# Weight sums spread over the second chunk, high parts moved to ScalarE, and PSUM banks exchanged in a two-mixer kernel

## The chip, the cores and the metric

The kernel runs on one core of a Trainium2 chip. The metric is the device time of one execution in microseconds; of several executions the median is given. The engines are named TensorE (PE in the profile, its weight loads PEld), VectorE (DVE), ScalarE (ACT), GpSimd (POOL) and SyncE (SP, whose queue issues the DMAs).

## What is computed

A linear attention, then two mixers, on a batch of 4 with 576 tokens of 512 channels. Inputs q, k, v are float32; most of the weights arrive as 64-bit floats.

```python
# attention: phi(x) = concat(exp(x@w_phi - m), exp(-(x@w_phi - m))), m = max|x@w_phi|
x  = num / den                                   # 4 x 576 x 512
# first mixer
u  = x + (x^T @ U @ V)^T                         # rank 32 over tokens
x  = u + max(u @ w_ch1, 0) @ w_ch2               # 512 -> 2048 -> 512
# second mixer
u  = x + (max(x^T @ w_tok1, 0) @ w_tok2)^T       # 576 -> 256 -> 576 over tokens
x  = u + max(u @ w_ch1', 0) @ w_ch2'             # 512 -> 1536 -> 512
```

## The kernel before

Every product is made of three matmuls. Each float32 operand is split (`split`, L94 to L98 with `cp` and `sub`) into a high part, a cast to fp32r (CAST, L96 on ScalarE or L98 on VectorE), and a low part, the subtraction of the cast from the operand (L101, on VectorE or POOL); a product is high x high, high x low and low x high, added up in a PSUM bank. The letters "a", "v", "p" in the calls of `split` choose ScalarE, VectorE or POOL.

The 64-bit weights are decoded on the chip by `load64`: a DMA brings a raw tile, ScalarE converts its two halves (L144 and L145), VectorE puts exponent, mantissa and sign together (L147, L150); the result, a tile w, is then split and its staging buffers become free.

The kernel has three phases.
- The attention with the token mix of the first mixer and 5 of the 16 slices of its channel part (to about 422 us). Its last results leave PSUM by `xT<-yp` (L498).
- The other 11 slices for eight half batches, `channel` (about 422 to 770 us): per slice a first product hp_b (12 matmuls of 288 columns), `relu_split` (L185 on ScalarE writes hhb, the high part; L186 on VectorE writes hlb, the low part) and the second product yb (12 matmuls into four banks). After each batch `tokmix2` does the token part of the second mixer (gp, gh, m2p).
- The channel part of the second mixer, `channelC`, called for five chunks of 256, 512, 512, 512 and 512 columns, named c0 to c4. The 12 slices of 128 hidden channels are taken in six pairs. The first chunk is plain: `one(p)` makes two first products hpc per pair, two relus, and `second(p)` multiplies them into the banks of yc. The other chunks go by `seven(p)`: the four products of a 2 x 2 block scheme are replaced by seven products of half the size (into banks named xc, yc, zc, vc), whose operands are parts of the activations (t0c to t6c, made by `token_mats` from uc) and weights or sums of weights. hbc, hac and u2c (L815 to L824) add the seven results together before the relus.

The weights of the pairs are loaded by `pair_weights`, while the second phase ends and chunk c0 runs: sh and sl hold seven high and low parts for a pair, vh and vl those of the second product. Entries 3 to 6 hold sums of weights: for the first two pairs (EARLY = 2) most are made in `pair_weights` (s, L672), for the others in `sums(p)` (s, L703, with casts on ScalarE and subtractions on VectorE), which before is called in chunk c0 after each pair. Its results are first read in chunk c1.

The order of instructions on each engine is set by the framework's scheduler, which lays them out ahead of time by its own estimates; `tc.issue_after(x)` keeps what is inside from standing ahead of x in that order. `gates` holds the two relu instructions behind which `token_mats` of a later chunk is laid. PSUM has eight banks; a pool that is opened first gets the lower ones, so the order of the pools psy (yc, yb, m2p: four banks), psh (hp_b, hpc, xc, yc's seven-product Y: two banks) and psg (two banks) decides which banks of the attention phase (psk bank 0, psx banks 1 to 5, psm 6 and 7) each gets.

Of the kernel before, what the change touches and what calls it, by code (L numbers as in the profile page):

```python
# [16 lines left out]
PSUM = bass.MemoryType.PSUM  # L17
# [14 lines left out]
NF2 = 12  # L32
# [5 lines left out]
EARLY = 2  # L38
# [51 lines left out]
def body(ctx, tc, kq, vd, w_phi, U, V, wm1, wt1, wt2, wm2, out):  # L90
# [12 lines left out]
    def split(src, hi, lo, eh, el):  # L103
        cp(eh, hi, src)
        sub(el, lo, src, f32(hi))
# [396 lines left out]
    for g in range(B * NPAIR):  # L502
        r = 5 * g
# [22 lines left out]
    for b in range(B):  # L526
        r = span * b + 5 * (NPAIR - 1) + O_TM
# [17 lines left out]
    with tc.using_default_side("right"):  # L545
# [1 line left out]
        extra.append(BX.enter_context(tc.tile_pool(name="rawx", bufs=RAWX, reuse_waits="tile")))  # L547
        bc = BX.enter_context(tc.tile_pool(name="bc", bufs=1, reuse_waits="tile"))
        b2 = BX.enter_context(tc.tile_pool(name="b2", bufs=2, reuse_waits="tile"))
    psy = ctx.enter_context(tc.tile_pool(name="psy", bufs=1, space=PSUM, reuse_waits="tile"))  # L550
    PB = ExitStack()
    psh = ctx.enter_context(tc.tile_pool(name="psh", bufs=2, space=PSUM, reuse_waits="tile"))
    psg = PB.enter_context(tc.tile_pool(name="psg", bufs=1, space=PSUM, reuse_waits="tile"))

    nB = NF1 - NA
# [69 lines left out]
    for t in range(NT):  # L625
        w = load64(wt1[:, t], P, 256, f"t1_{t}")
# [3 lines left out]
    for j in range(2):  # L630
        for k in range(2):
            sl = slice(k * N, (k + 1) * N)
# [46 lines left out]
    def pair_weights(p):  # L679
        sh, sl = [wc[p].tile([P, 7, 256], F32R, name=f"{t}{p}") for t in ("sh", "sl")]  # L680
        vh, vl = [wc[p].tile([P, 2, C], F32R, name=f"{t}{p}") for t in ("vh", "vl")]
        wa = loadc(2 * p, 0, p).rearrange("p (a k) -> p a k", a=2)
        split(wa, sh[:, 0:2], sl[:, 0:2], "a", "p")
        wb = loadc(2 * p + 1, 0, p)
        for k, i in enumerate((6, 2)):
            split(wb[:, k * 256 : (k + 1) * 256], sh[:, i], sl[:, i], "v", "p")
        if p < EARLY:
            sums3(p, wa, wb, sh, sl)
        for i in range(2):
            w = loadc(2 * p + i, 1, p)  # L690
            split(w, vh[:, i], vl[:, i], "av"[i], "pv"[i])
        return sh, sl, vh, vl

    wC = [pair_weights(p) for p in range(NF2 // 2)]
# [57 lines left out]
    gates = []  # L752
# [5 lines left out]
    def channelC(sl_, nm, plain):  # L758
# [4 lines left out]
        if plain:  # L763
            uh, ul = [pt.tile([P, NC, HM], F32R, tag=f"t{5 + i}", name=f"u{i}{nm}")[:, :, :n] for i in range(2)]
            split(u, uh, ul, "a", "v")
        else:
            with tc.issue_after(gates[0]), tc.issue_after(gates[1]):
                m = token_mats(u, h, nm)
        res = []
        for i in range(2):  # L770
            r = stc.tile([P, 2, 2 * HM], F32, tag="raw", name=f"res{nm}_{i}")[:, :, :n]
# [4 lines left out]
        def one(p):  # L776
            sh, sl = wC[p][:2]
            hs = []
            for i in range(2):
                hp = psh.tile([P, 512], F32, tag="m", name=f"hp{nm}_{p}_{i}")[:, :n]  # L780
                g = []
                for c in range(NC):
                    k = ((0, 1), (6, 2))[i][c // 2]
                    cs = slice((c % 2) * P, (c % 2 + 1) * P)
                    g += [(sh[:, k, cs], uh[:, c]), (sh[:, k, cs], ul[:, c]), (sl[:, k, cs], uh[:, c])]
                group(hp, g)
                hh, hl = hidden(2 * p + i, n, f"{nm}_{p}_{i}")
                r = relu_split(hp, hh, hl)
                if p == 3:
                    gates[:] = r  # L790
                hs.append((hh, hl))
            return hs

        def product(o, w, wi, ti, start):
# [8 lines left out]
        def seven(p):  # L803
            w = wC[p]
            pm = f"{nm}_{p}"
            X, Y = [psh.tile([P, 512], F32, tag="m", name=f"{t}{pm}")[:, :h] for t in ("x", "y")]
            Z, V = [psc.tile([P, 512], F32, tag=t, name=f"{t}{pm}")[:, :h] for t in ("z", "v")]
            product(X, w, 0, 0, True)
            e = pc.tile([P, HM], F32, tag="e", name=f"e{pm}")[:, :h]
            cp("a", e, X)  # L810
            product(Y, w, 4, 4, True)
            product(Z, w, 3, 3, True)
            product(V, w, 5, 5, True)
            u2 = pc.tile([P, HM], F32, tag="u2", name=f"u2{pm}")[:, :h]
            nc.vector.tensor_add(u2, Y, e)  # L815
            hb = pc.tile([P, 2 * HM], F32, tag="hb", name=f"hb{pm}")[:, :n]
            nc.vector.tensor_add(hb[:, h:], V, u2)
            nc.vector.tensor_add(hb[:, h:], Z, hb[:, h:])
            product(X, w, 1, 1, False)
            product(V, w, 2, 6, False)  # L820
            product(Z, w, 6, 2, False)
            nc.vector.tensor_add(hb[:, :h], V, u2)
            ha = pc.tile([P, HM], F32, tag="ha", name=f"ha{pm}")[:, :h]
            nc.vector.tensor_add(ha, Z, u2)  # L824
            (ah, al), (bh, bl) = hs = [hidden(2 * p + i, n, f"{pm}_{i}") for i in range(2)]
            relu_split(X, ah[:, :h], al[:, :h])
            relu_split(ha, ah[:, h:], al[:, h:])
            relu_split(hb, bh, bl)
            return hs

        def second(p, hs):
# [8 lines left out]
        prev = None  # L840
        for p in range(NF2 // 2):
            hs = one(p) if plain else seven(p)
            if plain:
                sums(p)
            if prev is not None:
                second(*prev)
            prev = (p, hs)
# [70 lines left out]
```

## Time and profile before

| what | value |
|---|---|
| median of 3 runs | 1084.78 us (1083.85 to 1087.3) |
| profiled execution | 1084.62 us |
| its span on the core | 1082.6 us |
| mean granted TensorE clock | 0.985 |
| TensorE busy | 1028.5 us, 95% of the span |
| VectorE busy | 673.5 us, 62% |
| ScalarE busy | 448.8 us, 41% |
| POOL busy | 238.7 us, 22% |

The profile records one execution. A time line gives for each group of like instructions the start, the busy time, engine, source line, operation, output and inputs and, in brackets, how long the engine was idle just before and whose end released it. The granted clock is a share of TensorE's full 2.4 GHz; half of it is the lower level of 1.2 GHz. Span and run differ by 2.0 us, which lie outside what the engines record.

### The profile page before, as it was taken

The page shows a single profiled execution, that of the slowest core. Times are in us where ns is not written, and L with a number is a line of the kernel's source. Part 1 is how long each engine was busy: PE and PEld are TensorE (multiplying, and loading weights), DVE is VectorE, ACT ScalarE, POOL GpSimd, SP SyncE. Part 2 cuts the span into 40 slices and gives each one's busy share as a digit, 9 for nine tenths or more (in the row PEclk, how much of TensorE's full clock was granted, in tenths as well). Part 3 has the DMA queues.
Part 4 walks back from the last instruction along what each step waited for, and adds up shares of the span by engine and source line. Part 5 has one row for each costly group of instructions (what it writes and reads, how often), then busy time and mean ns, then how long its engine had stood idle before and what let it go on. Part 6 is the DMA issues. An engine that isn't in the chain of part 4 may idle for free.

```text
span 1082.6 us, 17812 instructions
## 1 busy us (share of the span) xinstructions
PE 1028.5 (95%) x6960; PEld 952.2 (88%) x6960; DVE 673.5 (62%) x1221; ACT 448.8 (41%) x1049; POOL 238.7 (22%) x186
## 2 busy tenths in 40 slices
PE   8988999999989898999999999999988999999998
PEld 6767899899879787999999999998887889889887
DVE  7788987998898598743223223328899663543633
ACT  6676666756565566532112112114663221312211
POOL 3216565545545234100000000003240000000000
PEclk9998999999999999999999999999999999999999
DMA  7452323232221487410200200202753011030201
GB/s 213 151 157 58 102 56 92 71 98 71 75 78 24 128 283 230 153 60 22 89 23 22 88 22 2 88 1 80 245 157 108 1 64 55 1 117 1 78 2 39
DMA packets 62340, 92.16 MB, mean 85 GB/s; under 512 B 14512, under 2 KB 42928, under 8 KB 62256
## 3 DMA queue, kind: packets, MB, share of 16 engines
q1 hardware_dynamic: 62256, 91.03, 26.9%
q8 instruction: 54, 0.88, 0.3%
q14 instruction: 30, 0.25, 0.1%
HBM read 71.99 MB, written 18.95 MB: 84 GB/s over the span
## 4 chain that ended last, share of the span: by engine, by line
PE 69%; DVE 14%; ACT 6%; DMA 6%; issue 3%; POOL 2%; SPq 0%; DVEq 0%; ACTq 0%; POOLq 0%
PE yc L108 13%; PE yb L108 11%; PE hp_b L108 11%; PE hp_a L108 4%; PE yp L108 3%; PE pp L108 3%; PE zc L108 3%; PE vc L108 3%; PE kvp L108 3%; PE xc L108 3%; PE gp L108 2%; PE nm L108 2%; PE m2p L108 2%; PE dT L361 2%; DVE w_b L147 1%
## 5 line engine op out<-in xcount | busy, mean ns | idle before, releaser
L186 DVE SCALAR_TENSOR_TENSOR hlb<-hp_b,hhb 128x288 fp32r<-128x288 f32 x88 | 40.0, 456 | 158.5 <-ACT hhb L185 158.5
L185 ACT ACTIVATE hhb<-hp_b 128x288 fp32r<-128x288 f32 x88 | 36.1, 410 | 204.3 <-PE hp_b L108 201.6
L108 PE MATMUL hp_b<-uhb,wh_b 128*128 128x288 f32 x352 | 104.6, 299 | 3.4 <-DVE xT L498 3.4
L108 PE MATMUL hp_b<-ulb,wh_b 128*128 128x288 f32 x352 | 104.6, 297 | 0.0
L108 PE MATMUL hp_b<-uhb,wl_b 128*128 128x288 f32 x352 | 104.6, 297 | 0.0
L108 PE MATMUL yb<-hlb,wh_b 128*128 128x288 f32 x352 | 97.6, 297 | 2.1 <-DVE hlb L186 2.0
L108 PE MATMUL yb<-hhb,wl_b 128*128 128x288 f32 x352 | 97.1, 295 | 0.0
L101 POOL TENSOR_TENSOR sl<-w_c,sh 128x256 fp32r<-128x256 f32 (+1 forms) x18 | 23.8, 1340 | 332.2 <-DVE sh L98 292.1
L108 PE MATMUL yc<-hlc,vh 128*128 128x512 f32 (+1 forms) x240 | 88.3, 373 | 0.0
L108 PE MATMUL yc<-hhc,vl 128*128 128x512 f32 (+1 forms) x240 | 88.2, 372 | 0.0
L108 PE MATMUL yc<-hhc,vh 128*128 128x512 f32 (+1 forms) x240 | 81.9, 377 | 0.1
L101 POOL TENSOR_TENSOR qel<-qe,qeh 128x640 fp32r<-128x640 f32 (+1 forms) x48 | 71.3, 1496 | 25.9 <-ACT qeh L96 10.8
L108 PEld LDWEIGHTS hp_b<-uhb,wh_b 128*128 128x128 f32 x352 | 66.7, 190 | 4.8 <-DVE xT L498 3.6
L108 PEld LDWEIGHTS yb<-hlb,wh_b 128*128 128x128 f32 x352 | 66.1, 188 | 3.1 <-DVE hlb L186 3.0
L108 PE MATMUL yb<-hhb,wh_b 128*128 128x288 f32 x352 | 68.1, 296 | 0.6 <-ACT hhb L185 0.5
L108 PEld LDWEIGHTS hp_b<-ulb,wh_b 128*128 128x128 f32 x352 | 66.9, 190 | 0.1
L108 PEld LDWEIGHTS hp_b<-uhb,wl_b 128*128 128x128 f32 x352 | 66.7, 190 | 0.0
L108 PEld LDWEIGHTS yb<-hhb,wl_b 128*128 128x128 f32 x352 | 66.3, 188 | 0.0
L293 DVE TENSOR_REDUCE km<-pp 128x4 f32<-128x512 f32 x80 | 54.6, 683 | 13.4 <-PE pp L108 13.1
L101 POOL TENSOR_TENSOR kel<-ke,keh 128x512 fp32r<-128x512 f32 x36 | 48.6, 1361 | 64.2 <-ACT keh L96 62.7
L101 DVE TENSOR_TENSOR kd<-pp,km 128x512 f32<-128x512 f32 x80 | 54.4, 682 | 0.7
L108 PEld LDWEIGHTS yb<-hhb,wh_b 128*128 128x128 f32 x352 | 53.8, 188 | 1.1 <-ACT hhb L185 1.1
(249 smaller groups left out, 3056.5 us busy)
## 6 DMA issues: line engine op xcount, KB each, us to landing
raw_c<-in_wm_dram SPq DMA_DIRECT2D x24, 512.0 KB, 4.4
raw_b<-in_wm_dram SPq DMA_DIRECT2D x22, 512.0 KB, 4.6
kq<-in_kq_dram SPq DMA_DIRECT2D x80, 128.0 KB, 2.2
raw_a<-in_wm_dram SPq DMA_DIRECT2D x10, 512.0 KB, 4.3
rec<-rD SPq DMA_DIRECT2D x32, 144.0 KB, 3.2
uD<-xT SPq DMA_DIRECT2D x8, 576.0 KB, 3.4
sD<-xT SPq DMA_DIRECT2D x8, 576.0 KB, 5.3
x<-sD SPq DMA_DIRECT2D x8, 576.0 KB, 5.1
```

The costliest lines, as they stand in the source:

```text
L101: return ENG[e].tensor_tensor(out=o, in0=a, in1=b, op=ALU.subtract)
L108: nc.tensor.matmul(o, l, r, start=start, stop=stop, skip_group_check=True)
L147: nc.vector.scalar_tensor_tensor(out=wi, in0=wi, scalar=3, in1=r, op0=ALU.logical_shift_left, op1=ALU.bitwise_or)
L185: a = nc.scalar.activation(hh, hp, AF.Relu)
L186: v = nc.vector.scalar_tensor_tensor(out=hl, in0=hp, scalar=0.0, in1=f32(hh), op0=ALU.max, op1=ALU.subtract)
L293: nc.vector.tensor_reduce(out=m, in_=pv, op=ALU.max, axis=AX.X, apply_absolute_value=True)
L361: nc.tensor.transpose(tp[:, o : o + r], ds["q", g, t][:r, j, :], ident[:r, :r])
```

## The change

Five edits:
1. The pool psh is opened ahead of psy: the first products hp_b get banks 0 and 1, yb and yc banks 2 to 5. Before it was 4 and 5, and 0 to 3.
2. In `pair_weights` the casts of the second weight tile's two halves (sh entries 6 and 2) and of the second vh tile go to ScalarE. Before they were on VectorE. The subtractions stay where they were.
3. In chunk c0 `sums(p)` is called for the first two pairs only. Those of pairs 2 to 5 are queued in chunk c1, each in `seven(p - 2)` behind the last two relus of that pair.
4. The gates are taken anew in each chunk at pair 3 and dropped after use, so that `token_mats` of a chunk stands behind pair 3 of the chunk just in front. Before, those of chunk c0 served for all chunks.
5. In `one` the gates are set after both slices of pair 3.

```diff
--- before.py
+++ after.py
@@ -547,9 +547,9 @@
         extra.append(BX.enter_context(tc.tile_pool(name="rawx", bufs=RAWX, reuse_waits="tile")))
         bc = BX.enter_context(tc.tile_pool(name="bc", bufs=1, reuse_waits="tile"))
         b2 = BX.enter_context(tc.tile_pool(name="b2", bufs=2, reuse_waits="tile"))
-    psy = ctx.enter_context(tc.tile_pool(name="psy", bufs=1, space=PSUM, reuse_waits="tile"))
     PB = ExitStack()
     psh = ctx.enter_context(tc.tile_pool(name="psh", bufs=2, space=PSUM, reuse_waits="tile"))
+    psy = ctx.enter_context(tc.tile_pool(name="psy", bufs=1, space=PSUM, reuse_waits="tile"))
     psg = PB.enter_context(tc.tile_pool(name="psg", bufs=1, space=PSUM, reuse_waits="tile"))
 
     nB = NF1 - NA
@@ -683,12 +683,12 @@
         split(wa, sh[:, 0:2], sl[:, 0:2], "a", "p")
         wb = loadc(2 * p + 1, 0, p)
         for k, i in enumerate((6, 2)):
-            split(wb[:, k * 256 : (k + 1) * 256], sh[:, i], sl[:, i], "v", "p")
+            split(wb[:, k * 256 : (k + 1) * 256], sh[:, i], sl[:, i], "a", "p")
         if p < EARLY:
             sums3(p, wa, wb, sh, sl)
         for i in range(2):
             w = loadc(2 * p + i, 1, p)
-            split(w, vh[:, i], vl[:, i], "av"[i], "pv"[i])
+            split(w, vh[:, i], vl[:, i], "a", "pv"[i])
         return sh, sl, vh, vl
 
     wC = [pair_weights(p) for p in range(NF2 // 2)]
@@ -766,6 +766,7 @@
         else:
             with tc.issue_after(gates[0]), tc.issue_after(gates[1]):
                 m = token_mats(u, h, nm)
+            gates.clear()
         res = []
         for i in range(2):
             r = stc.tile([P, 2, 2 * HM], F32, tag="raw", name=f"res{nm}_{i}")[:, :, :n]
@@ -786,9 +787,9 @@
                 group(hp, g)
                 hh, hl = hidden(2 * p + i, n, f"{nm}_{p}_{i}")
                 r = relu_split(hp, hh, hl)
-                if p == 3:
-                    gates[:] = r
                 hs.append((hh, hl))
+            if p == 3:
+                gates[:] = r
             return hs
 
         def product(o, w, wi, ti, start):
@@ -825,7 +826,12 @@
             (ah, al), (bh, bl) = hs = [hidden(2 * p + i, n, f"{pm}_{i}") for i in range(2)]
             relu_split(X, ah[:, :h], al[:, :h])
             relu_split(ha, ah[:, h:], al[:, h:])
-            relu_split(hb, bh, bl)
+            r = relu_split(hb, bh, bl)
+            if p == 3:
+                gates[:] = r
+            if nm == "c1" and p + 2 < NF2 // 2:
+                with tc.issue_after(r[0]), tc.issue_after(r[1]):
+                    sums(p + 2)
             return hs
 
         def second(p, hs):
@@ -840,7 +846,7 @@
         prev = None
         for p in range(NF2 // 2):
             hs = one(p) if plain else seven(p)
-            if plain:
+            if plain and p < EARLY:
                 sums(p)
             if prev is not None:
                 second(*prev)
```

What the scheduler makes of it is shown at three places.

VectorE in the middle of chunk c1, before. hlc1_1_1 means the low part for chunk c1, pair 1, second slice; s3 and s4 are sums of pairs 3 and 4, ttc2 and uc2 the parts of chunk c2:
```order
L736 TENSOR_TENSOR ttc2_10565<-uc2_10560 128x512
L817 TENSOR_TENSOR hbc1_1_10110<-vc1_1_10081,u2c1_1_10108 128x256
L703 TENSOR_TENSOR s3_2_9755<-s3_1_9751 128x256
L736 TENSOR_TENSOR uc2_10560<-uc2_10560 128x2x256
L818 TENSOR_TENSOR hbc1_1_10110<-zc1_1_10080,hbc1_1_10110 128x256
L703 TENSOR_TENSOR s3_2_9755<-s3_2_9755,s3_0_9750 128x256
L703 TENSOR_TENSOR s3_1_9751<-s3_0_9750,s3_1_9751 128x256
L101 TENSOR_TENSOR sl3_9383<-s3_2_9755,sh3_9382 128x256
L703 TENSOR_TENSOR s3_0_9750<-s3_0_9750,s3_2_9755 128x256
L101 TENSOR_TENSOR sl3_9383<-s3_2_9755,sh3_9382 128x256
L101 TENSOR_TENSOR sl3_9383<-s3_1_9751,sh3_9382 128x256
L703 TENSOR_TENSOR s4_0_9826<-sh4_9428,sl4_9429 128x512
```
Three more rows of sums follow, and then hlc1_2_0, which empties the bank of xc1_2.

VectorE at the same place of chunk c1, after:
```order
L186 SCALAR_TENSOR_TENSOR hlc1_1_1_10083<-hbc1_1_10056,hhc1_1_1_10082 128x512
L703 TENSOR_TENSOR s3_0_10090<-sh3_9382,sl3_9383 128x512
L703 TENSOR_TENSOR s3_1_10091<-sh3_9382,sl3_9383 128x256 x2
L816 TENSOR_TENSOR u2c1_2_10162<-yc1_2_10133,ec1_2_10142 128x256
L186 SCALAR_TENSOR_TENSOR hlc1_1_0_10081<-hac1_1_10078,hhc1_1_0_10080 128x256
L186 SCALAR_TENSOR_TENSOR hlc1_2_0_10189<-xc1_2_10132,hhc1_2_0_10188 128x256
L703 TENSOR_TENSOR s3_2_10095<-s3_1_10091 128x256
L818 TENSOR_TENSOR hbc1_2_10164<-vc1_2_10135,u2c1_2_10162 128x256
L703 TENSOR_TENSOR s3_2_10095<-s3_2_10095,s3_0_10090 128x256
L703 TENSOR_TENSOR s3_1_10091<-s3_0_10090,s3_1_10091 128x256
L819 TENSOR_TENSOR hbc1_2_10164<-zc1_2_10134,hbc1_2_10164 128x256
```
The sums of pair 3 now start behind hlc1_1_1, with hlc1_2_0 after their first rows, and ttc2 has left this place; it stands behind u2c1_4.

ScalarE and VectorE at the end of the second phase, as a difference (- before, + after). The names are without their numbers of pair: hhb_1_7 and hlb_1_7 are the relu of slice 7 in the last half batch, sh the high parts of a pair of chunk weights. First ScalarE:
```order
 L96 CAST sh_9280<-w_c_0_9286 128x512
+L185 ACTIVATE hhb_1_7_8912<-hp_b_1_7_8899 128x288
 L144 ACTIVATE w_c_1_9318<-raw_c_1_9316 128x512
-L185 ACTIVATE hhb_1_7_8912<-hp_b_1_7_8899 128x288
 L145 ACTIVATE r_c_1_9319<-raw_c_1_9316 128x512
+L96 CAST sh_9280<-w_c_0_9296 128x256 x2
 L96 CAST sh_9280<-s_9306 128x256 x2
+L185 ACTIVATE hhb_1_8_8941<-hp_b_1_8_8928 128x288
```
The casts have come in, one relu has moved ahead of a decode and the next one ahead of another.

VectorE at the same place:
```order
 L147 SCALAR_TENSOR_TENSOR w_c_0_9296<-w_c_0_9296,r_c_0_9297 128x512
 L150 SCALAR_TENSOR_TENSOR w_c_0_9296<-raw_c_0_9294,w_c_0_9296 128x512
-L98 CAST sh_9280<-w_c_0_9296 128x256 x2
+L186 SCALAR_TENSOR_TENSOR hlb_1_7_8913<-hp_b_1_7_8899,hhb_1_7_8912 128x288
 L672 TENSOR_TENSOR s_9306<-w_c_0_9296 128x256
-L186 SCALAR_TENSOR_TENSOR hlb_1_7_8913<-hp_b_1_7_8899,hhb_1_7_8912 128x288
 L672 TENSOR_TENSOR s_9306<-s_9306,w_c_0_9286 128x256
```
The two casts and a sum no longer stand between the decode and hlb.

ScalarE in the plain chunk c0, where hhc_2_1 is the relu of pair 2, second slice:
```order
-L185 ACTIVATE hhc_2_1_9670<-hpc_2_1_9657 128x256
 L96 CAST sh_9428<-w_c_0_9434 128x512
 L145 ACTIVATE r_c_1_9457<-raw_c_1_9454 128x512
+L185 ACTIVATE hhc_2_1_9670<-hpc_2_1_9657 128x256
+L96 CAST sh_9428<-w_c_0_9444 128x256 x2
 L144 ACTIVATE w_c_1_9466<-raw_c_1_9464 128x512
 L145 ACTIVATE r_c_1_9467<-raw_c_1_9464 128x512
```
The relu stands two places later, and the casts of the weights behind it.

## Rows read from the trace of the kernel before

**Rows 1.** The page's busy line: busy us (share of span) xinstructions of each engine.
```profile
PE 1028.5 (95%) x6960; PEld 952.2 (88%) x6960; DVE 673.5 (62%) x1221; ACT 448.8 (41%) x1049; POOL 238.7 (22%) x186
```
**Rows 2.** Stretches: length, busy us (xinstructions) of each engine, PEclk, DMA share, GB/s.
```profile
768.00:820.00 52.00, 47.80 (x368) 44.93 (x367) 47.92 (x84) 30.82 (x59) 23.59 (x16) 1.00 0.52 164
820.00:866.00 46.00, 41.26 (x252) 36.52 (x251) 34.12 (x91) 13.18 (x34) 0.00 (x0) 0.96 0.18 58
841.50:845.50 4.00, 4.00 (x19) 3.67 (x19) 4.00 (x11) 1.90 (x7) 0.00 (x0) 0.57 0.01 4
866.00:1083.00 217.00, 212.35 (x1309) 189.31 (x1308) 98.06 (x203) 46.28 (x99) 0.00 (x0) 0.99 0.13 44
```
**Rows 3.** Waits of PE, 735 to 866 us: total us, times, longest us.
```profile
PE xc L108 <- DVE hlc L186: 3.6, 2, 2.8
PE hpc L108 <- DVE hlc L186: 2.3, 3, 1.3
PE yb L108 <- DVE hlb L186: 1.5, 2, 1.0
PE zc L108 <- DVE t3c L101: 1.3, 1, 1.3
```
**Rows 4.** Time line of PE in chunk c1: start us, us, instruction [idle before <-releaser].
```profile
840.51 0.50 PE L108 MATMUL xc<-t0c,sh 128*128 128x256 f32 x2 [2.80 <-DVE hlc L186]
...
854.82 0.40 PE L108 MATMUL yc<-t4c,sh 128*128 128x256 f32 x2
...
855.53 1.10 PE L108 MATMUL yc<-hhc,vh 128*128 128x512 f32 x4
856.46 0.40 PE L108 MATMUL xc<-t1c,sh 128*128 128x256 f32 x2
```
**Rows 5.** Time line of DVE in chunk c1.
```profile
830.44 1.34 DVE L703 TENSOR_TENSOR s<-sh,sl 128x512 f32<-128x512 f32 x3
834.21 0.69 DVE L736 TENSOR_TENSOR ttc<-uc 128x512 f32<-128x512 f32 x1 [2.42 <-DMA uc<-u2D]
...
838.43 0.68 DVE L703 TENSOR_TENSOR s<-sh,sl 128x512 f32<-128x512 f32 x1
...
840.04 0.41 DVE L186 SCALAR_TENSOR_TENSOR hlc<-xc,hhc 128x256 fp32r<-128x256 f32 x1
```
**Rows 6.** Groups by shape, 725 to 866 us: busy us, mean ns | idle before.
```profile
L96 ACT CAST sh<-s 128x256 fp32r<-128x256 f32 x24 | 9.4, 404 | 20.1 <-DVE s L703 15.3 <-DVE s L672 4.6
L96 ACT CAST vh<-w_c 128x512 fp32r<-128x512 f32 x6 | 3.7, 618 | 2.2 <-DVE w_c L150 2.0
L98 DVE CAST sh<-w_c 128x256 fp32r<-128x256 f32 x12 | 3.4, 325 | 0.8 <-PE yb L108 0.7
L98 DVE CAST vh<-w_c 128x512 fp32r<-128x512 f32 x6 | 2.7, 451 | 0.0
```
**Rows 7.** Time line of DVE in chunk c0: casts of weight halves.
```profile
785.28 0.97 DVE L98 CAST sh<-w_c 128x256 fp32r<-128x256 f32 x2
...
796.48 0.48 DVE L98 CAST sh<-w_c 128x256 fp32r<-128x256 f32 x2
```
**Rows 8.** Time line of POOL at the same two places.
```profile
784.60 1.30 POOL L101 TENSOR_TENSOR sl<-w_c,sh 128x512 fp32r<-128x512 f32 x1 [8.49 <-ACT sh L96]
...
796.84 1.87 POOL L101 TENSOR_TENSOR sl<-w_c,sh 128x256 fp32r<-128x256 f32 x2 [0.83 <-DVE sh L98]
```
**Rows 9.** Time line of PE at the start of the second phase.
```profile
425.37 0.61 PE L108 MATMUL hp_b<-uhb,wh_b 128*128 128x288 f32 x1 [3.40 <-DVE xT L498]
...
431.28 0.40 PE L108 MATMUL yb<-hlb,wh_b 128*128 128x288 f32 x1 [0.50 <-DVE hlb L186]
```
**Rows 10.** Time line of ACT there: the first relu.
```profile
428.85 0.40 ACT L185 ACTIVATE hhb<-hp_b 128x288 fp32r<-128x288 f32 x1
```
**Rows 11.** Time line of DVE there.
```profile
429.19 1.67 DVE L150 SCALAR_TENSOR_TENSOR w_b<-raw_b,w_b 128x512 int32<-128x512 int32 x1
430.78 0.81 DVE L186 SCALAR_TENSOR_TENSOR hlb<-hp_b,hhb 128x288 fp32r<-128x288 f32 x2
```

## The prediction

> **What bounds the kernel now.** I read the page's busy line first [rows 1]: TensorE is busy 1028.5 us of a span of 1082.6 us, VectorE 673.5 and ScalarE 448.8. So the matmuls set the time, and an edit gains only what it takes out of TensorE's idle time or out of time at a reduced clock. The profiled execution took 1084.62 us, 0.16 below the median of 1084.78, so a sum made against it stands for the median too.
>
> Then I asked where the idle time lies. All that the change moves is issued after about 735 us, with one exception at the start of the second phase (below). In the table of stretches [rows 2] the last 217 us, chunks two to four of the channel mixer, have TensorE at 98% (212.35 of 217.00): nothing is to be had there, and the order there hardly changes. The plain chunk (768 to 820 us) has 47.80 of 52.00, and VectorE is busy 47.92 of the same 52.00, POOL 23.59 and ScalarE 30.82. The second chunk's first part (820 to 866) has 41.26 of 46.00. So some 9 us of idle TensorE lie in these two stretches.
>
> The waits of TensorE there [rows 3] name VectorE nearly every time: xc behind hlc (3.6 us in two waits, the longest 2.8), hpc behind hlc (2.3 in three), yb behind hlb (1.5 in two), zc behind t3c (1.3). Each is a short VectorE instruction that stands late in VectorE's queue, behind work which nobody on TensorE needs yet.
>
> **Part 1, the sums and the parts of the next chunk (second chunk).** The longest wait is read in three steps. TensorE starts the product into xc at 840.51 after 2.80 us of idling on hlc, which still has to empty that bank [rows 4]. VectorE reaches that hlc only at 840.04 [rows 5]. Ahead of it in its queue stands the first subtraction of the parts of chunk two, ttc<-uc at 834.21, which idles VectorE for 2.42 us on the load of uc; then the sums of pairs three and four (s rows such as the three at 830.44 and the one at 838.43). In the changed order both go: ttc2 stands behind u2c1_4, four pairs later, and hlc1_2_0 has only the first sums of the next pair ahead of it (the order rows above). With the wait goes a second cost: after it TensorE runs 841.5 to 845.5 at a granted clock of 0.57 [rows 2], a mix of the 1.2 and the 2.4 GHz level. 4.00 us x (1 - 0.57) = 1.7 us. Together 2.8 + 1.7 = 4.5. I take **-4.4**; the low end of the gain is -2.4, the 2.42 us idle of VectorE alone, if the queue of sums still holds hlc for the rest. The other xc wait, 3.6 - 2.8 = 0.8, has the sums of pair two ahead of its hlc and goes the same way: **-0.6** (0 to -0.8).
>
> Does it come back later? The four pairs' sums are still to be done in this chunk. A pair costs VectorE two instructions of 512 columns at 0.68 (s at 838.43; hlc of the same width) and 17 of 256 at 0.41 (hlc at 840.04): 1.4 + 7.0 = 8.3 us counted by whole durations, somewhat less as they overlap. A pair costs TensorE seven products of six matmuls at 0.71 (854.82 to 855.53) and 24 wide matmuls at 0.93 per four (855.53 to 856.46) [rows 4]: 5.0 + 5.6 = 10.6 us. Between the relus of pair p and yc of pair p+2, which is the first to use its sums, stand six products and 24 wide matmuls: 4.3 + 5.6 = 9.9 us. The sums need at most 8.3. So the slack is 1.6 us or more for each pair, and no wait takes the place of the old one. What is next late is the start of the chunk: u2c1_0 stands behind the four additions of the plain chunk's results, t6c and sl1. That may leave half a microsecond to one of waiting; before it was there too, so I book nothing.
>
> **Part 2, high parts on ScalarE (end of the second phase, plain chunk).** VectorE gives up 12 casts of 128x256 at 325 ns (3.4 us) and 6 of 128x512 at 451 (2.7 us); ScalarE takes them at about its own 404 and 618 ns for these shapes [rows 6]: 12 x 0.404 + 6 x 0.618 = 8.6 us. Two thirds of that, four of six pairs, falls in 768 to 820: VectorE goes from 47.92 to about 43.9 of 52.00, ScalarE from 30.82 to about 36.5 [rows 2]. VectorE, the engine that TensorE waits for there, gets 4 us of room; ScalarE keeps 15. The waits in that stretch are hpc behind hlc 2.3, zc behind t3c 1.3 and two below 0.4. I book about half of the two named, **-2.0**. The far end is -4.0 (all that VectorE sheds). On the other side, each relu of ScalarE now can stand behind a cast that itself waits for the decode on VectorE, and POOL's subtraction waits for that cast before it frees the staging buffer; twelve casts that are 0.08 us longer and six that are 0.17 us longer put 2.0 us of delay on this ring, of which I let three quarters reach TensorE: **+1.5** is the near end.
> In the second phase's tail the two casts of sh1 leave the place ahead of hlb3_1_7, and on ScalarE the relu hhb3_1_7 passes a decode instruction. The waits of yb behind hlb are 1.5 in all [rows 3]: **-1.0** (0 to -1.5).
>
> One rule bears on it. The trace shows two of these casts taking 0.97 us together at 785.28, inside a POOL subtraction that began at 784.60, and 0.48 at 796.48 with POOL idle until 796.84 [rows 7, 8]. The Trainium skill (SBUF — State Buffer, section Who interferes with whom) says that VectorE and GpSimd share a port pair which one of them holds for a whole instruction, a VectorE cast in its two-port mode among the takers, and that ScalarE never waits for it. By that rule the six pairs of casts would shed up to 6 x 0.49 = 2.9 us more, and the stage would gain up to that again; but by the same rule the decode instructions with two SBUF inputs, which stay on VectorE, would meet POOL at other places, so that the gain may only move. The sum is made without it.
>
> **Part 3, first products on other banks (start of the second phase).** Before, hp_b waits 3.40 us for xT<-yp, the read-out of the bank that it gets, and starts at 425.37 [rows 9]. Its new banks are free, the first at once, the second after an earlier xT. That looks like a gain of 3.4. But who waits for hp_b? ScalarE's first relu hhb runs at 428.85, behind a row of weight decodes and casts that do not depend on TensorE [rows 10]; VectorE runs the decode w_b<-raw_b at 429.19 for 1.67 and then hlb at 430.78 [rows 11]; and TensorE waits for that hlb until 431.28 [rows 9]. The queues of ScalarE and VectorE are in the same order in both kernels there. So hp_b comes early, TensorE idles behind it instead of ahead of it, and yb with hlb still starts at 431.28. The gain is 0 by this chain. An idle stretch there may bring a lower clock for the yb that follows, as the stall in the second chunk did for 1.7 us. I take **+0.5**, between -0.5 (the wait of 0.50 on hlb, if hlb comes a little earlier) and +1.7.
>
> **Part 4, the gates.** They move the parts of chunks two to four behind the fourth pair's last relu of the chunk in front. In the stretch from 866 on TensorE has 2% to lose [rows 2], and two pairs, 2 x 10.6 us, are left to do the parts (four subtractions and seven splits, 11 instructions like ttc<-uc at 0.69 [rows 5], 7.6 us of VectorE). They are hidden by VectorE's idle time there (98.06 of 217.00 busy): 0. If that cover were gone, a chunk's start would wait a few us.
>
> Sum: -4.4 - 0.6 - 2.0 - 1.0 + 0.5 = -7.5. 1084.6 - 7.5 = **1077 us**.
>
> **The rivals.**
> A. The banks do free the start of the second phase: the 3.4 us go, and the slow clock after them with about 1.5. In the sum -4.9 stands for +0.5: 1084.6 - 8.0 - 4.9 = about 1072. For it speaks the size of the wait; against it the rows of ScalarE and VectorE, which end later and don't wait for hp_b.
> B. ScalarE becomes the late one in the plain chunk and the tail: part 2 gives +1.5 and 0 in place of -2.0 and -1.0. 1084.6 - 4.4 - 0.6 + 1.5 + 0.5 = about 1081.6. For it: in the changed order relus stand one or two places later behind casts that wait for the decode. Against: ScalarE has 21 of 52 us free.
> C. The change does not do what it says in the second chunk: hlc is no longer held by the load, but the sums that were done in the plain chunk's shadow now hold it a little at each pair; only the 2.4 of part 1 stays. 1084.6 - 2.4 - 2.0 - 1.0 + 0.5 = about 1080.
> D. Slower: the sums, queued behind the relus of pair p, are not done when TensorE reaches yc of pair p+2. That decides once the chain of relu, sums, casts on ScalarE and splits takes more than 9.9 us, 1.6 us beyond my 8.3. Then each of four pairs has a wait like the one of 2.8 with its 1.7 of slow clock: 4 x 4.5 = 18 us more, against 5.0 saved and 2.5 elsewhere: 1084.6 - 5.0 + 18.0 - 2.5 = about 1095. For it: sums alternate between VectorE and ScalarE, and each hop costs. Against: in the 10.6 us of a pair VectorE is needed for 8.3 at most and ScalarE has little else.
>
> **How the numbers follow.** My forecast 0.66, A 0.06, B 0.16, C 0.07, D 0.05. A measurement of this kernel can tell 0.3% from no change, 3.3 us: faster is below 1081.5. The forecast, A and most of C lie there, B sits on the line and I give half of it to either side: 0.66 + 0.06 + 0.05 + 0.08 = 0.85 faster, 0.02 + 0.08 = 0.10 the same, D 0.05 slower. The range: the favourable ends give -4.5 - 0.8 - 4.0 - 1.5 - 0.5 = -11.3, 1073; B and the unfavourable ends of part 1 and 3 reach 1082.5. 1072.5 to 1082.5 leaves out A, D and a little of B and C, some 0.15.
>
> **What would show it right or wrong.** Right: no wait over 1 us of xc behind hlc between 820 and 866 and no clock below 0.9 there; ttc2 late in the second chunk with no idle ahead of it; VectorE at about 44 of 52 in the plain chunk; hp_b starting before 424 but yb with hlb still at about 431. Wrong: waits of yc behind casts or splits of the sums at each of four pairs (D); hpc or yb waits that name ScalarE or POOL in the plain chunk (B); yb with hlb before 430 (A).

## The result and the profile after

The changed kernel took 1075.94 us (median of 4 runs, 1074.05 to 1077.88) against 1085.27 of the kernel before (median of 4); the ratio is 0.9913 with an interval of 0.9886 to 0.9940. The forecast was 1077 with 1072.5 to 1082.5. Run again beside later experiments, it took 1077.74 (12 runs) against 1080.72 (17 runs), a ratio of 0.9960 (0.9938 to 0.9982). The two intervals barely touch: the changed kernel repeated within 2 us, while the kernel before was 4.6 us faster in the second series. The traces show one reason why the time alone is a poor judge here: the first phase, whose instructions are the same in both and in the same order, reached its last matmul, a yp, anywhere between 418.3 and 424.2 us in the profiled executions. So the comparison is made from that last yp on. Matmuls come in the same order there in long stretches, and the start of the same matmul can be taken in every trace:

| stretch (us, from starts of the same matmuls) | before | after | after, second profile |
|---|---|---|---|
| last yp to the second half batch's first hp_b | 39.84 | 40.77 | 41.86 |
| to the last half batch's first hp_b | 259.71 | 259.71 | 259.68 |
| to the last batch's first gp | 39.23 | 38.62 | 38.74 |
| to chunk c1's first xc (plain chunk) | 54.50 | 51.87 | 51.96 |
| to the last yc (chunks c1 to c4) | 263.01 | 257.22 | 257.16 |
| sum | 656.29 | 648.19 | 649.40 |

From the last yp on the change is worth 8.1 us (6.9 in the second profile), 7.5 was forecast. The other 2.2 us between the two profiled spans lie in the first phase and are no work of the change. The second series gives 3.0 us in time, at most 6.7 by its interval, which is less than the traces give. The kernel before has one profile only, from the first series, so it is not shown whether its first phase ended earlier in the second series or whether the change was worth less there.

One border of the table is not the same in both. Before, all six matmuls of the second chunk's product zc on t3c come ahead of its first xc; after, five of them come behind it. They start 0.12 us apart, so 0.6 us of the plain chunk's 2.6 are matmuls that only moved across the border. Like for like the plain chunk is 2.0 shorter and the rest 6.4.

The page's busy line after answers to [rows 1]:

```profile
PE 1021.4 (95%) x6960; PEld 948.1 (88%) x6960; DVE 670.5 (63%) x1203; ACT 455.5 (42%) x1067; POOL 240.4 (22%) x186
```

Stretches of after, for [rows 2]; the first is the plain chunk, taken 0.2 us ahead of the two matmuls of the table. Columns: length, busy us of PE, PEld, DVE, ACT, POOL, then PEclk:

```profile
758.35:810.22 51.87, 48.76 (x367) 45.48 (x366) 47.56 (x74) 37.60 (x73) 24.05 (x16) 1.00 0.62 202
...
820.00:866.00 46.00, 46.00 (x295) 41.46 (x294) 34.64 (x89) 16.84 (x40) 0.00 (x0) 1.00 0.11 42
841.50:845.50 4.00, 4.00 (x32) 3.82 (x31) 3.94 (x11) 1.43 (x4) 0.00 (x0) 1.00 0.01 2
```

From 820 to 866 us TensorE is busy 46.00 of 46.00 us (41.26 before) and the granted clock is 1.00 throughout. That stretch starts further into the second chunk than before, behind a wait of 1.6 us which the next list shows. The same plain stretch before:

```profile
760.40:814.90 54.50, 50.41 (x371) 46.33 (x370) 48.53 (x82) 34.18 (x62) 23.75 (x16) 1.00 0.60 192
```

Waits of TensorE after, 725 to 870 us, for [rows 3] (total us, times, longest us):

```profile
PE xc L108 <- DVE u2c L816: 1.6, 1, 1.6
PE yb L108 <- DVE hlb L186: 1.5, 2, 1.0
PE hpc L108 <- DVE hlc L186: 1.3, 2, 0.8
PE hpc L108 <- DVE u1c L101: 0.8, 1, 0.8
PE m2p L108 <- ACT gh L185: 0.6, 1, 0.6
PE hpc L108 <- POOL sl L101: 0.3, 1, 0.3
```

The waits of xc on hlc (3.6) and of zc on t3c (1.3) are gone, hpc on hlc has fallen from 2.3 to 1.3. Three waits are new or larger: xc on u2c, 1.6, hpc on u1c, 0.8 instead of 0.2, and m2p on gh, 0.6. yb on hlb is as long as before. Before also had three smaller waits at the start of the second chunk, which are gone:

```profile
PE vc L108 <- DVE hbc L817: 0.5, 1, 0.5
...
PE yc L108 <- DVE u2c L815: 0.4, 1, 0.4
PE zc L108 <- DVE hac L824: 0.3, 1, 0.3
```

### The profile page after: what moved, and what is told of

Its sections match the earlier page's. It is cut to its first block, busy times and chain, and to the rows that moved or that the text cites. A ratio compares the mean times of both kernels' runs of the same rounds, so it can differ in the third digit from the quotient of the medians.

```text
span 1072.3 us, 17821 instructions
## 1 busy us (share of the span) xinstructions
PE 1021.4 (95%) x6960; PEld 948.1 (88%) x6960; DVE 670.5 (63%) x1203; ACT 455.5 (42%) x1067; POOL 240.4 (22%) x186
## 4 chain that ended last, share of the span: by engine, by line
PE 75%; DVE 11%; ACT 5%; issue 3%; DMA 3%; POOL 2%; SPq 0%; DVEq 0%; ACTq 0%; POOLq 0%
PE yc L108 14%; PE yb L108 12%; PE hp_b L108 12%; PE hp_a L108 4%; PE nm L108 4%; PE pp L108 4%; PE kvp L108 4%; PE yp L108 3%; PE vc L108 3%; PE zc L108 3%; PE xc L108 3%; PE gp L108 2%; PE m2p L108 2%; PE dT L361 1%; DMA raw_a<-in_wm_dram 1%
```

## The experiments

Each run was profiled once; the stretches are those of the table above. The times of the kernels that ran only once, 1070 to 1088 us, hold the first phase's variation and are not compared. For the chunks the last two lines of the table are added (last batch's first gp to the end: 317.51 before, 309.09 after, 309.12 in the second profile), since some orders move matmuls across the border between them (all kernels with the casts on ScalarE have five matmuls more behind it).

**The parts one by one, on the kernel before.** Banks alone:

```diff
-    psy = ctx.enter_context(tc.tile_pool(name="psy", ...))
     PB = ExitStack()
     psh = ctx.enter_context(tc.tile_pool(name="psh", ...))
+    psy = ctx.enter_context(tc.tile_pool(name="psy", ...))
```

> The kernel before with the banks exchanged alone. My theory (the queues of ScalarE and VectorE hold the second phase's start, not the bank): hp_b starts right behind the last yp instead of 3.7 us later, but the first yb with hlb starts as long after the last yp as before (9.6 us), TensorE now idles 4 us on hhb, and the half clock falls on yb; from the last yp to the second half batch 0.5 to 0.9 us more than before, nothing else moves. Rival (the bank held it): the first yb with hlb comes 3 us earlier and the second half batch 3 to 5 us earlier.

Time line of PE in this kernel at the start of the second phase, the last yp and the first yb with hlb:

```profile
422.60 0.30 PE L108 MATMUL yp<-hha,wl_a 128*128 128x288 f32 x1
...
432.15 0.61 PE L108 MATMUL yb<-hlb,wh_b 128*128 128x288 f32 x1 [0.63 <-DVE hlb L186]
```

They are 9.55 us apart. Before, the last yp is this one, and yb with hlb follows at 431.28 [rows 9], 9.60 later:

```profile
421.68 0.29 PE L108 MATMUL yp<-hha,wl_a 128*128 128x288 f32 x1
```

The bank has not brought yb nearer. The second half batch starts 41.57 us after the last yp, 1.7 later than before, where 0.5 to 0.9 was expected; the chunks take 316.95, within 0.6 of before. The banks alone gain nothing.

The high parts on ScalarE alone:

```diff
-            split(wb[...], sh[:, i], sl[:, i], "v", "p")
+            split(wb[...], sh[:, i], sl[:, i], "a", "p")
...
-            split(w, vh[:, i], vl[:, i], "av"[i], "pv"[i])
+            split(w, vh[:, i], vl[:, i], "a", "pv"[i])
```

> The kernel before with the high parts on ScalarE alone. My theory: plain chunk 2 to 3 us shorter, end of the second phase 0.6 shorter, the wait of xc on hlc in the second chunk stays at 2 us or more, so 2.5 to 3.5 us less in all behind the second phase. Rival (the plain chunk gains because the sums have left it): under 1 us there.

Plain chunk 51.97 (2.5 less, 2.0 like for like), last half batch 0.5 less: as the theory had it. The rest of the chunks gained as well, 313.44 in all against 317.51: 4.1, more than the 2.5 to 3.5 expected. Two of the waits, 765 to 870 us:

```profile
PE xc L108 <- DVE u2c L815: 2.9, 1, 2.9
...
PE xc L108 <- DVE hlc L186: 1.2, 1, 1.2
```

The wait of xc on hlc stayed, at 1.2 instead of the 2 or more that I expected, and a wait on u2c of 2.9 came up at the chunk's start. The likely reading is that the plain chunk ends earlier and VectorE, which is behind, is waited for there.

The sums alone:

```diff
-            relu_split(hb, bh, bl)
+            r = relu_split(hb, bh, bl)
+            if nm == "c1" and p + 2 < NF2 // 2:
+                with tc.issue_after(r[0]), tc.issue_after(r[1]):
+                    sums(p + 2)
...
-            if plain:
+            if plain and p < EARLY:
                 sums(p)
```

> The kernel before with the sums queued behind the relus of the second chunk alone; the parts of chunk two still stand ahead of hlc of pair 2, and so the load they wait for. Theory that the load is the greater half of the long wait: a wait of xc on hlc of 1 to 3 us stays in the second chunk and the gain there is under 3.5 us. Rival that the sums ahead of hlc are: the wait is gone and the gain is 5 to 6 us.

And the gates alone:

```diff
                 m = token_mats(u, h, nm)
+            gates.clear()
...
-            relu_split(hb, bh, bl)
+            r = relu_split(hb, bh, bl)
+            if p == 3:
+                gates[:] = r
```

> The kernel before with the gates of the activation parts alone; the sums of pairs 3 and 4 still stand ahead of hlc of pair 2. Theory that the load of uc is the greater half: VectorE no longer idles 2.4 us, the long wait of xc on hlc shrinks to under 1 us, with it the low clock, and the second chunk gains 3 to 4.5 us. Rival that the sums hold it: the wait stays above 2 us and the gain is under 1.5 us.

The sums alone brought the chunks to 310.33 (7.2 less), though 3 us of their plain chunk ran at a granted clock of 0.50; the gates alone brought them to 312.33 (5.2 less). The sums' run came out as its rival had it (with a larger gain), the gates' run as its theory, and together they leave no "greater half": each part alone takes the wait of 2.8 away. VectorE with the sums alone, where ttc still waits for its load ahead of hlc of pair 2:

```profile
830.87 0.69 DVE L736 TENSOR_TENSOR ttc<-uc 128x512 f32<-128x512 f32 x1 [0.84 <-DMA uc<-u2D]
...
835.51 0.42 DVE L186 SCALAR_TENSOR_TENSOR hlc<-xc,hhc 128x256 fp32r<-128x256 f32 x1 [0.34 <-ACT hhc L185]
```

and with the gates alone, where the sums still stand ahead of it:

```profile
832.35 0.74 DVE L703 TENSOR_TENSOR s<-sh,sl 128x256 f32<-128x256 f32 x2
833.51 0.42 DVE L186 SCALAR_TENSOR_TENSOR hlc<-xc,hhc 128x256 fp32r<-128x256 f32 x1 [0.41 <-ACT hhc L185]
```

In both VectorE gets to hlc and then waits 0.3 to 0.4 us for ScalarE's hhc: VectorE is no longer late. The stall of before needed both, the idling on the load (2.42 us there, 0.84 with the sums alone) and the sums in the queue [rows 5].

Sums and gates together, without banks and casts (the two diffs above, with both lists of lines behind `r = relu_split`):

> The kernel before with the sums and the gates of the change, without the banks and without the casts on ScalarE. If the parts act at their own places: plain chunk as before (54 to 55 us from the last token product to the first product of the second chunk), second chunk as with the sums alone (67.3 us, within 0.4, against 69.07 after), so from the end of the first phase to the end only 0 to 1.5 us more than after. Rival (the casts are worth their 2.5 us on top): 2 to 3 us more than after.

310.32 from the last batch's first gp to the end, the same as with the sums alone: as far as one profile of each can tell, the gates add nothing to the sums. The plain chunk takes 53.37, 1.1 less than before and less than the 54 to 55 expected, though no cast has left VectorE: sums and gates give room there too. From the last yp it is 648.97, 0.8 more than after, which has other banks. So the casts are worth 310.32 - 309.09 = 1.2 on top in the chunks, not the 4.1 that they gave alone. The parts don't add up: 4.1 + 7.2 + 5.2 = 16.5 singly, 8.4 together.

**The banks again, on the changed kernel:** the first diff backwards.

> The changed kernel with the banks as before. By the rows of before and of the runs with the old banks: from the last yp to the second half batch 39.8 to 40.8 us against 40.8 to 41.6 with the new ones, so the new banks cost about 1 us, and the rest is as after. Rival: the new banks help or are neutral, 40.8 or more here.

From the last yp to the second half batch 39.87, and 647.8 to the end, 0.4 less than after and 1.6 less than its second profile. (The plain chunk takes 52.33 here, with about 3 us at a granted clock of 0.50.) Over all profiles with ScalarE's old queue the six with the old banks lie at 39.83, 39.84, 39.84, 39.87, 40.55 and 40.78 (mean 40.1) and the five with the new ones at 40.77, 40.90, 41.46, 41.57 and 41.86 (mean 41.3). So the new banks cost about 1.2 us while that queue stands. About half of it goes with the clock: four of the six with the old banks, those at 39.83 to 39.87, have a granted clock of 0.50 there for about 3 us, and the other two, at 40.55 and 40.78, and all five with the new banks for about 7.

**What holds the start of the second phase.** ScalarE's first relu stands behind the decodes of weight slices 7 and 8, which are used some 20 us later. In this experiment the slices 7 to 10 and the token weights are queued behind the first relus instead:

```diff
-    wB = [load_w(...) for f in range(nB)]
+    wB = [load_w(...) for f in range(7)]
+    todo = list(range(7, nB))
...
+    def more(r):
+        f = todo.pop(0)
+        with tc.issue_after(r[0]), tc.issue_after(r[1]):
+            wB.append(load_w(...))
+            if not todo:
+                token_weights()
...
-            relu_split(hp[:, :n], hh, hl)
+            r = relu_split(hp[:, :n], hh, hl)
+            if todo:
+                more(r)
```

> The changed kernel, in which the decode of the weight slices 7 to 10 and of the token weights is queued behind the first relus of the second phase instead of ahead of them. Theory (ScalarE's and VectorE's queue of decodes, and not PSUM, holds the start of the second phase): the wait of yb on hhb falls from 4.1 to under 1 us, no half clock follows, and the second half batch starts 4 to 6 us earlier after the last yp than after. Rival (the start is held by something else, the bank's read-out or the loads): under 1.5 us earlier, or later because weights are missing.

PE of this kernel, the last yp and the first listed yb with hlb, and then ACT's first relu:

```profile
418.42 0.30 PE L108 MATMUL yp<-hha,wl_a 128*128 128x288 f32 x1
...
422.27 0.29 PE L108 MATMUL yb<-hlb,wh_b 128*128 128x288 f32 x1
```

```profile
420.35 0.41 ACT L185 ACTIVATE hhb<-hp_b 128x288 fp32r<-128x288 f32 x1 [5.96 <-PE hp_b L108]
```

ScalarE is now the one that waits, 5.96 us for hp_b, and yb with hlb comes 3.9 us after the last yp instead of 9.6. The second half batch starts after 34.97 us, 5.8 earlier than after; of that 1.4 goes back in the following half batches (261.09), all of it in the second one, where yb waits 0.6 for VectorE's additions of the first one's results. This profile's plain chunk is 1.2 longer (53.06), with a granted clock of 0.83 between 760 and 768 us; the timed run's profile has 51.93 there, so that is not the kernel's.

> The same kernel as in the run with the weights of slices 7 to 10 decoded later, now timed. From the last yp to the end it took 644.9 us against 648.2 after: if this holds, 3 us below the changed kernel and 11 below before, ratio to before about 0.990 to 0.985. Rival: the 1.2 us of half clock at the start of the plain chunk and the 1.4 us in the second phase's body come in most executions, and the gain is nearer to 2.

1071.17 us (6 runs, 1070.67 to 1073.77), ratio to before 0.9914 (0.9893 to 0.9935); 643.85 from the last yp. In the same series the changed kernel gave

> The changed kernel once more, beside the two others and before. Second chunk, end of the second phase and the last three chunks should repeat to 0.1 us (69.07, 38.6 and 188.15 us); the plain chunk should be 51.9 or, with a half-clock stretch at its start, 53.1; from the last yp to the second half batch 40.7 to 41.5. The time in all varies with the first phase, by up to 5 us.

1077.74 us (12 runs). So this version beats both kernels, by 6.6 and 9.6 us where 3 and 11 were expected. Its banks as before:

> The same with the banks as before. Theory (in the changed kernel the banks are worth nothing because ScalarE's queue holds the start; with that queue free they decide): hp_b starts 1 to 3.5 us after the last yp, and the second half batch 1.5 to 3.5 us later than with the new banks. Rival (the read-out by xT is early now that VectorE is free, and the bank is worth under 0.7 us).

1072.20 us, not to be told from 1071.17 by time. By the trace hp_b still waits, but only this long:

```profile
419.90 0.40 PE L108 MATMUL hp_b<-uhb,wh_b 128*128 128x288 f32 x1 [0.55 <-DVE xT L498]
```

and the second half batch starts at 35.74 instead of 34.93 to 34.97. With the queue free the new banks are worth 0.8 us. The theory, 1.5 to 3.5 us, fell, and the rival with its "under 0.7" is nearly right: most of the old wait of 3.40 for the bank was itself VectorE's queue, in which xT stood behind decodes.

**The lead of the sums (rival D as a dose).** The sums one pair ahead instead of two:

```diff
-            if nm == "c1" and p + 2 < NF2 // 2:
+            if nm == "c1" and 2 <= p + 1 < NF2 // 2:
                 with tc.issue_after(r[0]), tc.issue_after(r[1]):
-                    sums(p + 2)
+                    sums(p + 1)
```

> The changed kernel with the sums queued one pair ahead instead of two: sums of pair p+1 behind the relus of pair p. A dose for rival D of the prediction. Theory (the lead of two pairs is what keeps the sums hidden; they take about 7 to 8 us of alternating VectorE and ScalarE work): TensorE waits at each of four pairs for splits or casts of the sums, 3 to 7 us each, the second chunk 12 to 28 us longer than after. Rival (there is so much room that even one pair's lead is enough): under 4 us longer.

From the first xc of c1 to the end 268.06 against 257.22, 10.8 more: under the 12 to 28 expected, far over the 4 of the rival. PE in that chunk:

```profile
846.01 1.47 PE L108 MATMUL yc<-hhc,vh 128*128 128x512 f32 x4 [1.95 <-ACT hhc L185]
...
860.52 1.20 PE L108 MATMUL yc<-hhc,vh 128*128 128x512 f32 x4 [1.78 <-ACT hhc L185]
...
873.60 1.20 PE L108 MATMUL yc<-hhc,vh 128*128 128x512 f32 x4 [1.23 <-ACT hhc L185]
```

The stalls come 14.5 and 13.1 us apart, but name the relu and not the sums, and the scheduler gave the matmuls another order. Their sum is 5.0 us, under half of the loss; other waits there (hlc 1.5) and a stretch at a lower granted clock (0.77 from 843 to 850) are part of the rest. How the loss comes about was not settled.

**The wait that the change brought in.** The additions of a chunk's results, queued behind the next chunk's first u2c:

```diff
-        for c in range(NC):
-            nc.vector.tensor_add(res[c], yp[c][:, :n], res[c])
...
+            v = nc.vector.tensor_add(u2, Y, e)
+            if left:
+                with tc.issue_after(v.ins):
+                    left.pop()()
+                setup()
```

> The changed kernel with the additions of a chunk's results (resc) queued behind u2c of the next chunk's first pair. Theory (the 1.6 us wait of xc on u2c at the start of the second chunk comes from the four additions, t6c and the last split ahead of u2c): the wait falls below 0.5 us and the second chunk gets 1.2 to 1.8 us shorter. Rival (the additions hold the banks of the second product, which now waits for them): no gain or a loss.

The waits of this kernel, 805 to 825 us:

```profile
PE xc L108 <- DVE u2c L821: 0.7, 1, 0.7
PE xc L108 <- ACT ec L96: 0.5, 1, 0.5
```

against 1.6 in one piece. The chunks take 309.13 instead of 309.09: nothing gained, where 1.2 to 1.8 was expected. The rival's mechanism (the banks of the second product) doesn't show either. The wait on u2c is 0.9 shorter, and another appears behind it: the scheduler now puts xc on t1c right behind xc on t0c, and it waits for ScalarE's copy ec of that product.

## Why the prediction was right

Like for like, from the last yp on, the four terms -5.0, -2.0, -1.0 and +0.5 came out as -6.4, -2.0, -0.6 and +0.9. That their sum, -8.1 (-6.9 in the second profile), lies so near to -7.5 is in part luck: the misses go both ways. So does the time: 1077 was reckoned from a kernel before at 1084.6, and in the second series that kernel took 1080.72. Where a step failed, it is named under its term.

**The second chunk, -5.0 predicted.** Chunks c1 to c4 got 5.8 shorter (6.4 like for like) and the stall with its slow clock is gone: [rows 4] had 2.80 us at 840.51, and after has 46.00 of 46.00. The mechanism held, but two statements around it did not. The bound of -2.4 supposed that the load's share could go and the sums' stay; the runs showed that either repair alone takes the whole stall away. And "I book nothing" for the chunk's start missed a wait of 1.6, which the row after shows, with VectorE's queue ahead of it:

```profile
817.75 0.51 PE L108 MATMUL xc<-t0c,sh 128*128 128x256 f32 x2 [1.61 <-DVE u2c L816]
```

```profile
815.02 1.41 DVE L856 TENSOR_TENSOR resc<-yc,resc 128x256 f32<-128x256 f32 x4
816.35 0.68 DVE L101 TENSOR_TENSOR t6c<-uc,t6c 128x512 fp32r<-128x512 f32 x1
816.95 0.42 DVE L101 TENSOR_TENSOR sl<-s,sh 128x256 fp32r<-128x256 f32 x1
817.28 0.42 DVE L816 TENSOR_TENSOR u2c<-yc,ec 128x256 f32<-128x256 f32 x1
```

The prediction named just these instructions ahead of u2c and put them at half a microsecond to one, as before. Before, 0.8 on hlc and the three smaller waits above made 2.0 us at this place, so the idling there changed its names and hardly its length; the -0.6 booked for the wait on hlc was mostly not gained. It did not see that a plain chunk which ends earlier reaches these instructions earlier. With sums and gates alone, without the casts, the waits there are 0.3 on u2c and 0.8 on hlc. The casts alone gave 2.0 in the plain chunk and 2.1 behind it; with sums and gates alone the long stall was already gone and the plain chunk 1.1 shorter, which left 1.2 for the casts.

**The gates, 0 predicted.** Chunk c2 is 0.5 us shorter, with the sums alone too; c3 and c4 take 123.71 us from the last second product of c2 to the end in both kernels. The gates do take the load's idling out of the way (after, ttc starts at 854.51 with none ahead of it), but the sums alone reached the same total.

**The plain chunk, -2.0 predicted, -2.6 measured (2.0 like for like).** The size is in part luck: all of it was booked on the casts, and sums and gates without casts give 1.1 there, for which the prediction had no term. The price of the casts was right: ScalarE took

```profile
L96 ACT CAST vh<-w_c 128x512 fp32r<-128x512 f32 x12 | 7.4, 617 | 6.8 <-DVE w_c L150 6.7
L96 ACT CAST sh<-w_c 128x256 fp32r<-128x256 f32 x12 | 4.3, 409 | 0.0
```

409 and 617 ns against the 404 and 618 that the prediction took. Waits on hlc and t3c fell by 2.3 us as forecast. The statement that VectorE would be at 44 of 52 us there was wrong: in the matched stretch it is busy 47.56 of 51.87, 92%, where it was 48.53 of 54.50, 89%. Eleven casts left that stretch (4.2 us), but two sums came in (0.8), and the subtractions for t3c and u1c, both with two inputs in SBUF, took 1.3 us longer together. The groups of VectorE's decode, 725 to 866 us, first before, then after:

```profile
L150 DVE SCALAR_TENSOR_TENSOR w_c<-raw_c,w_c 128x512 int32<-128x512 int32 x21 | 20.3, 969 | 0.2
L147 DVE SCALAR_TENSOR_TENSOR w_c<-w_c,r_c 128x512 int32<-128x512 int32 x21 | 16.2, 771 | 4.6 <-ACT r_c L145 4.0 <-ACT w_c L144 0.6
```

```profile
L150 DVE SCALAR_TENSOR_TENSOR w_c<-raw_c,w_c 128x512 int32<-128x512 int32 x21 | 19.0, 904 | 0.3
L147 DVE SCALAR_TENSOR_TENSOR w_c<-w_c,r_c 128x512 int32<-128x512 int32 x21 | 18.2, 865 | 4.0 <-ACT r_c L145 2.6 <-ACT w_c L144 1.4
```

The 42 decodes took 36.5 us before and 37.2 after, though 18 instructions have left the engine beside them; POOL's time in the plain stretch went from 23.75 to 24.05. The Trainium skill (SBUF — State Buffer, section Who interferes with whom) says that a VectorE instruction with two SBUF inputs contends with a GpSimd instruction that reads SBUF, and that ScalarE never waits for that port. The extra 2.9 us which the prediction drew from that rule did not come (the plain chunk gained 2.0 in all); that the contention moves to other two-input instructions, as the prediction allowed, agrees with the slightly longer decodes and the longer t3c and u1c, and no run separates it further.

**The tail of the second phase, -1.0 predicted, -0.6 and -0.5 measured.** The wait of yb on hhb (0.5) went, the one on hlb did not. It moved from slice 7 to slice 8. First before, then after:

```profile
750.06 0.40 PE L108 MATMUL yb<-hlb,wh_b 128*128 128x288 f32 x1 [0.95 <-DVE hlb L186]
```

```profile
751.55 0.40 PE L108 MATMUL yb<-hlb,wh_b 128*128 128x288 f32 x1 [1.01 <-DVE hlb L186]
```

VectorE gets to that hlb after another decode, a split and a sum of the chunk weights:

```profile
749.77 0.68 DVE L150 SCALAR_TENSOR_TENSOR w_c<-raw_c,w_c 128x512 int32<-128x512 int32 x1
750.37 0.42 DVE L101 TENSOR_TENSOR sl<-s,sh 128x256 fp32r<-128x256 f32 x1
750.71 0.42 DVE L672 TENSOR_TENSOR s<-w_c,w_c 128x256 f32<-128x256 f32 x1
751.04 0.45 DVE L186 SCALAR_TENSOR_TENSOR hlb<-hp_b,hhb 128x288 fp32r<-128x288 f32 x1
```

The step that failed is the one that stopped at the next relu and did not ask what is late behind it.

**The banks, +0.5 predicted, +0.9 and +2.0 measured** (1.2 over all profiles; the far end was +1.7). The reason held to the tenth. PE, ACT and DVE after:

```profile
419.47 0.30 PE L108 MATMUL yp<-hha,wl_a 128*128 128x288 f32 x1
419.61 0.30 PE L108 MATMUL hp_b<-uhb,wh_b 128*128 128x288 f32 x1
...
427.10 1.33 PE L108 MATMUL yb<-hhb,wh_b 128*128 128x288 f32 x4 [4.11 <-ACT hhb L185]
429.07 0.61 PE L108 MATMUL yb<-hlb,wh_b 128*128 128x288 f32 x1 [0.64 <-DVE hlb L186]
```

```profile
426.62 0.43 ACT L185 ACTIVATE hhb<-hp_b 128x288 fp32r<-128x288 f32 x1
```

```profile
427.00 1.65 DVE L150 SCALAR_TENSOR_TENSOR w_b<-raw_b,w_b 128x512 int32<-128x512 int32 x1
428.57 0.81 DVE L186 SCALAR_TENSOR_TENSOR hlb<-hp_b,hhb 128x288 fp32r<-128x288 f32 x2
```

hp_b starts right behind yp, the 3.40 us of waiting ahead of it [rows 9] have become 4.11 + 0.64 behind it, and yb with hlb comes 429.07 - 419.47 = 9.60 us after the last yp, before 9.60. Rival A falls with that. (Its sign, yb with hlb before 430, is met by the figure 429.07, but only because the last yp came 2.2 us earlier.) The size was too small because the slow clock now falls on more work:

```profile
425.30:428.50 3.20, 1.33 (x4) 0.98 (x4) 2.58 (x3) 2.67 (x6) 1.28 (x1) 0.50 0.98 304
428.50:431.00 2.50, 1.93 (x8) 1.93 (x9) 1.97 (x4) 1.20 (x2) 1.28 (x1) 0.50 0.61 182
```

These stretches of after have 0.50 where before the clock was back at 0.98 from 428.5 on. Before, the slow matmuls were hp_b, and ScalarE's first relu would have come no sooner had they been fast; after, they are yb, on the path.

**The other rivals.** B: no wait of hpc or yb names ScalarE in after's list, and of POOL only 0.3 as before; gh (0.6) is new and small. C would have left c1 with a small wait at each pair: none stands in the list. D: two pairs of lead are enough, since after's list has no wait for the sums; with one pair 10.8 us are lost, though the stalls there name the relu, so D's own mechanism was not seen.

One sum of the prediction is wrong: rival B with the unfavourable ends of parts 1 and 3 gives 1084.6 - 2.4 + 1.5 + 1.7 = 1085.4 and not 1082.5. The measured times lie far from that end. And the two casts of [rows 7] lie only partly inside POOL's subtraction [rows 8]: it ends at 785.90, they end at 786.25.

## What to carry to other kernels

When a matmul waits for a bank's read-out, ask first what the matmuls behind it wait for: a free bank only moves the idling if the next engine's queue is full, and pulling work that is needed 20 us later out of that queue gave 5.8 us at that place (4.3 to the end) where the bank cost about one. Compare stretches between the same matmuls, not whole times, where one phase varies by more than the change. And don't add the gains of parts that relieve the same engine: here 4.1, 7.2 and 5.2 made 8.4. And count the matmuls on both sides of a border before a stretch is compared.

## What the runs showed of the hardware

The first phase's end varied by 6 us (418.3 to 424.2) with the same instructions in the same order, while the six half batches behind it repeated to 0.04 us (259.68 to 259.72, except where the later decodes changed them). At the start of the second phase the granted clock fell to 0.50 in all eleven profiles in which TensorE idled 3.37 to 4.12 us in one piece there; with the decodes queued later, and waits of at most 0.6 us, it stayed at 1.00 in all three. Stalls of the same length did not always cost the same: in the plain chunk, after waits of 0.60 us on gh and 0.84 on u1c, the granted clock stayed at 1.00 in the changed kernel (its line above) and fell in the run with the later decodes, whose plain chunk was 1.2 us longer. The stretch there (PEclk behind POOL):

```profile
760.00:768.00 8.00, 6.47 (x30) 5.21 (x30) 7.93 (x9) 6.02 (x12) 6.49 (x4) 0.83 0.68 224
```
